# Attention and MoE on one core: the second, offset transpose of q becomes two copies that exchange partition halves

## The chip, the cores and the metric

The kernel runs on one core of one Trainium2 chip. The time is device microseconds of one execution. The profile is one execution of the program recorded by the hardware profiler; engines are named as in it: PE (matrix engine), PEld (its weight loads), DVE, ACT, POOL and SP. SP computes nothing here: it issues DMAs from its queue, one after the other, and an instruction that waits for a semaphore holds up all that stand behind it. PE, too, takes its instructions in the order in which they were written.

## The reference

Eight batches of twelve heads, 448 positions, head width 64; then one feed-forward layer over the 3584 rows that come out:

```python
scores = scale * np.matmul(q, k.transpose(0, 1, 3, 2))   # q, k, v: (8, 12, 448, 64), scale = 1/8
attn = np.maximum(scores, 0.0) ** 2 / S                   # S = 448, no softmax
x = np.matmul(attn, v)                                    # then (8*448, 768)
h = x @ w_in                                              # (768, 2048)
g = 0.5 * h * (1.0 + erf(h * inv_sqrt2))
out = g @ w_out                                           # (2048, 768)
```

Inputs and output are float32; the kernel computes with bfloat16 operands.

## The kernel before, in words

**Layout.** A batch `b` is worked on in three groups `g` of four heads. For the score products q and k must lie with the head width (64) on the partitions, so both are turned. Queries are loaded as 112 partitions with four chunks `c` of 64 columns each per head (`load_q`: row `p*4+c` of a head is chunk `c` of partition `p`); keys are loaded as 128 partitions. Batches 0 and 1 are turned on PE (`add_tk`, `add_tq`). Batches 2 to 7 are turned by DMA transposes on SP's queue (`add_T_dma`, line 660).

**The turned q, before.** One transpose takes 128 columns at a time, that is two chunks, and puts the first on partitions 0 to 63, the second on 64 to 127. A score product reads 64 partitions and must find all four chunks of a head there. So q is transposed twice per group: the "even" transpose starts at a chunk's edge, the "odd" one is offset by 64 columns. Both write into every other slot of `qT`, so that each half holds the four chunks side by side and a product reads one run of 448 columns (`moving = qT[r, n * KC : n * KC + S]`). The odd transpose reaches one chunk past its group, so it also waits for the next group's load; two memsets clear the two column blocks at q's ends. With one transpose of k that is nine transposes per batch, 54 in all (36 of q, 18 of k).

**Order.** Nothing is scheduled at run time. The string `ORDER` lists the operations of all engines, each word a letter for the engine (P = PE, A = ACT, D = DVE, G = POOL, S = SP) and a number (the operation's place in the order in which the code adds them). Each engine gets its words in that order. In batch 2 the nine operations 228 to 236 are k, q even, q odd of group 0 (228, 229, 230), of group 1 (231, 232, 233), and of group 2 (234, 235, 236). Written as k2.0 (batch 2, group 0) and so on, SP's queue before is

- q2.0 even, k2.0, q2.0 odd, k2.1, q2.1 odd, q2.1 even, q2.2 odd, q2.2 even, k2.2 (S229 S228 S230 S231 S233 S232 S236 S235, and S234 four lines further on).

**What waits for what.** A score block `(b, g, i)` (`fn_qk`, line 734, four products of 64x448) waits for its group's k and q transposes. There are seven blocks per group. P276 to P294 are the blocks of batch 2 group 0, P300 to P318 those of group 1, P324 to P342 those of group 2; PE runs them among feed-forward products (line 847, line 1259), in the order P285 (a block of group 0), P300, P303 (the first two of group 1). After each group come the products with v (line 795).

**Loads.** POOL issues all loads, in its own order, into one queue. Before loads that overwrite turned data POOL runs a *gate* (`add_gate`, line 701): a 16-column copy of `qT` that waits for the group's transposes, and so holds back the loads behind it. Around batch 2 POOL's order is: gate of group 0, two pieces of `w_out` (line 490), gate of group 1, a large piece of `w_out` (16 row blocks), then v, q of batch 3, **k of batch 2 group 2** (`G153`), and further loads. Each output block is stored by two DMAs on SP (line 1125), which stand in SP's queue between the transposes.

Of the kernel before, what the change touches and what calls it, by code (L numbers as in the profile page):

```python
# [9 lines left out]
BF16 = mybir.dt.bfloat16  # L10
AF = mybir.ActivationFunctionType

B, H, S, D = 8, 12, 448, 64
KC = 112
# [10 lines left out]
SLOTS = H * NC + 1  # L25
# [44 lines left out]
T_LOAD = 1.0  # L70

# [12 lines left out]
G0 G1 G3 G4 G1428 G7 G121 A10 P11 D13 G2 A16 P17 D12 P14 G117 D18 P42 P39 G6 P21 D15 P19 A43  # L84
G118 P36 D22 P33 A40 P23 G5 D20 P25 D41 P54 A37 G122 D24 Z1056 D26 A34 P66 P57 D38 A55 D44 G8
P63 P29 P27 A58 D67 P69 P51 D35 A64 P48 D30 P31 D65 A70 P45 D28 D32 A52 P78 D59 G9 P133 D46 A49
P108 D68 D47 P111 A79 P75 D134 P129 A109 D50 P81 P131 D56 A76 P102 D112 P84 G125 A82 D71 P72 D53
A103 G120 P60 D130 A85 D104 P93 A73 P135 A61 D110 A74 A62 P96 D132 P105 G124 P141 D83 D77 A97
P168 A94 D106 P165 P90 A142 G119 P143 D86 D113 A169 G126 D107 P114 A166 D80 P87 D98 A91 D95 P171
A144 D115 P137 A88 D92 A116 P99 D89 P156 A172 D136 P159 A100 D138 P145 G128 A157 A101 D160 P162  # L90
P186 D167 P174 A146 P251 D163 A175 P243 D158 A187 D176 G148 A252 D170 P183 P195 P189 G147 D173
A244 P259 G151 A196 D184 G154 P253 D161 A260 G150 D164 P139 A190 P198 A254 P180 P177 D140 A181
D199 P219 P216 P245 A178 G123 G127 A220 D217 P207 A179 P210 P204 D191 A246 P261 S229 A211 D208
P247 D182 A205 S228 D209 A262 D197 P213 P222 P192 D200 S230 A248 P263 D221 A223 D206 P249 D224
A264 D188 P255 D212 A250 P257 D193 A214 A256 D194 P265 D218 S231 A258 D185 P201 D215 A266 G237
S233 G239 P225 A202 S232 A203 P276 P279 P267 D226 S236 A277 A227 P291 D280 P288 P294 S235 A268
P356 G240 A295 D289 G238 P350 A357 G149 P348 G272 A292 A351 G153 P285 P300 P303 G270 A349 P354
G241 A301 P364 A304 A355 P312 P318 P362 A365 P370 D319 D281 A363 D296 P358 A313 D290 A286 P282
P306 A371 P315 P352 A359 D307 P360 A353 P376 A361 P368 A316 A377 D317 P372 D314 A369 D308 P366
D293 A373 P378 A283 A367 D284 P374 S234 A379 D390 P382 D278 S400 A375 D391 S402 D392 P380 D417  # L100
D418 D305 G242 G152 D302 S399 D287 G269 P327 P339 D320 P297 G271 D396 G155 A328 D383 P333 G274
P384 D381 G273 D298 A340 A299 D393 A334 D394 P330 P324 P309 D329 P387 D419 A331 D335 A385 S398
A310 D395 D311 S386 A325 P342 P336 S401 P321 D397 D388 A343 D332 P421 A322 D337 A323 S403 P423
D420 D338 D422 S406 P446 P443 D341 P449 P425 D424 D344 A450 S404 P427 G410 D444 G275 A426 G412
S405 D447 P429 D326 D428 P452 P455 P345 A456 D453 P440 P437 D445 P431 D430 A441 D560 P433 D346
A347 D432 P473 A438 P461 P470 D434 P509 G413 G407 G414 A471 D474 P513 D448 G409 A462 S545 D457
A510 G415 P479 D454 P476 P464 G408 A514 P519 D472 D442 G411 A465 D439 P517 A520 D477 P515 A480
D451 A518 S547 P485 P467 P458 S436 A468 P491 A516 S543 P511 D459 A486 D561 P523 S389 A492 D487
S549 A512 D460 P503 P494 P500 D563 A524 P525 D463 S541 A495 D466 P521 D469 A526 D481 P531 S548
D504 A522 D478 P527 A532 D501 P537 D475 S542 A528 D505 P529 D502 A538 D493 S546 P488 P497 P482  # L110
S544 A498 D489 P606 G556 P600 G550 G416 P535 A483 A530 G558 P533 D601 G551 A607 D484 A536 G553
D490 G552 P539 D496 G555 D499 P609 G559 P603 P506 G557 A604 D610 G554 P624 A534 P639 D562 P564
A540 D605 A507 P566 A640 D625 D565 D508 P615 P612 P618 D567 P568 A616 D613 P570 D617 A569 D611
D614 P572 S708 D619 P657 D571 P627 P636 S706 P574 D580 D573 A637 D620 P576 D608 A658 D575 S578
A628 P584 D581 S704 D638 D577 P586 D583 S579 D582 P630 D602 P633 P621 S707 D626 A634 D631 P651
A585 S710 P642 P588 D632 D587 A643 S705 D659 P590 D629 A652 A622 D641 P648 A623 D644 P666 P663
A589 S712 D653 P592 D635 D591 A664 S709 G713 P594 G714 A649 D667 D593 S711 P654 P660 P645 A655
D661 P769 P763 D595 P596 S598 D725 A770 G719 G721 A646 P672 D764 G715 D597 P674 G720 D665 D650
A673 G716 G717 A647 D656 P772 P778 P775 G718 D662 A675 P678 S867 A776 D779 P676 D668 A773 D771
P766 D777 P787 P669 S868 A767 D788 A679 P781 P790 A677 D774 P682 A670 D723 D768 P684 A782 A671  # L120
D724 A683 D765 P680 D783 A791 D780 P796 P799 P784 A681 S874 A800 D797 P793 P802 S435 P688 S869
D803 D804 S870 D798 D789 S872 D792 S873 S871 S875 G882 G722 A785 A685 P686 A794 A689 A786 P811
P823 P805 A687 P690 D795 A806 P692 A691 D824 P698 D726 A812 D807 A693 P696 D801 A699 P814 P817
P808 A697 A815 D818 P820 P906 G884 P694 A809 G876 G877 P702 D907 G883 A695 A810 G878 P700 G879
A821 G881 A703 P826 P829 D822 P912 A701 P727 A827 P729 D828 A728 D813 P731 A913 D730 A830 D816
P733 D819 D825 P921 D831 P909 P832 A910 D922 P918 P936 D732 G885 P735 D734 A833 G880 D911 A919
D834 P924 P915 A937 P737 D736 A916 D925 P930 P933 D938 P942 P739 D743 A931 D738 S741 D744 P747
A934 D745 D740 S742 P749 D917 S599 A748 D935 S979 P751 D914 A943 D920 D750 S983 P753 D944 A752
D746 S985 P755 D923 D926 D754 P757 D932 D908 S986 P939 P948 P927 D758 S978 A940 D949 P960 P945
D941 P835 A928 S980 D756 D950 A946 P759 A929 S761 D961 S982 D947 P957 P954 P951 A836 D760 S981  # L130
A958 D955 P963 P966 P839 D956 A952 S762 D953 S984 A967 P837 D959 A840 P969 D964 P972 P987 A838
D888 P841 A973 P843 D988 D965 A842 D989 P845 A970 D962 A844 D974 P847 D971 A846 D1067 P1002 D968
P990 P975 A1003 D991 A848 P993 P996 P851 D976 A994 A977 P999 D997 P1014 P1005 A852 D1004 P849
D995 D992 P853 D886 A850 D1068 P857 D998 A1000 A854 P855 D1015 A1006 D1001 P1017 D1007 P1026
P1008 D1070 A1027 D1018 P1029 A856 P1011 P859 A858 D1059 A1009 D1028 P863 D1019 A1030 A860 D1031
P865 A1012 D1060 A864 A1010 P1035 D887 P1047 P1020 D1016 A866 P861 A1048 P890 D1021 A1036 A862
D1063 D1022 P1023 P1041 P1044 A891 D1013 P892 A1024 D1042 P1053 A1045 D1025 P1050 P1032 D1069
A1051 D1054 P1038 P1071 A1033 D1062 P894 D1049 A1072 D1043 P1088 D893 A1039 P1073 A1034 D1066
A895 P1079 A1089 D1040 P1090 D889 P1096 P1075 D1091 P896 D1055 D1074 D1181 P1094 D1052 P1077
D897 P1092 P898 D1095 D1078 P1082 D1064 P1099 P900 D1061 D899 D1097 P902 D1083 D1100 P1105 D1080  # L140
D901 P1102 A1076 D1179 P1085 A1106 D1139 P1122 A1093 D1046 A1084 P1107 D1037 P1124 A1123 D903
S905 P1109 A1081 D1086 P1126 D1103 A1087 P1113 D1108 P1130 D1125 A1110 P1128 A1127 D1065 P1111
A1104 D1140 A1098 P1056 D1180 D1129 D1112 P1133 D1131 P1143 D1057 D1114 P1119 D1058 P1136 D1134
D1291 P1116 D1144 P1183 D1120 P1200 D1137 P1185 D1117 P1202 A1184 D1141 A1201 P1191 D1182 P1187
D1203 P1145 D1186 P1189 P1206 P1208 P1147 D1190 D1207 D1146 P1194 D1192 P1211 D1209 P1149 D1195
P1214 D1212 D1148 P1217 D1150 P1197 D1142 P1151 A1218 A1115 D1198 A1118 P1221 D1215 A1135 P1234
D1152 A1121 P1219 A1132 P1236 A1101 A1138 P1153 A1235 D1237 P1238 D1161 P1155 D1220 D1154 S1157
P1240 D1159 P1223 D1156 S1158 P1163 D1160 D1241 P1245 P1165 D1164 D1224 P1228 P1167 D1166 D1162
D1246 P1169 D1229 D1168 P1225 P1171 D1170 D1253 P1173 D1172 D1226 P1175 D1251 P1242 P1231 A1239
P1204 A1222 P1303 A1227 D1243 P1248 D1176 A1188 P1320 A1205 D1252 P1295 A1210 D1174 S1177 A1244  # L150
D1232 P1312 S904 A1199 D1292 P1255 S1178 A1230 D1249 A1296 D1254 A1313 P1297 D1293 A1193 P1314
A1196 P1299 A1256 P1257 A1233 D1298 A1213 D1315 A1216 P1301 P1316 D1258 P1318 P1261 D1319 P1259
D1302 D1304 D1294 P1309 D1262 P1323 A1260 A1250 P1263 D1310 A1247 D1324 P1306 D1321 P1265 D1264
D1307 P1326 P1329 P1346 D1327 P1331 D1271 P1267 A1347 D1272 A1330 P1350 P1348 D1268 P1333 P1275
D1349 D1266 S1269 D1273 P1277 S1270 D1276 P1279 D1274 D1332 D1278 P1352 P1335 A1280 P1281 P1283
# [239 lines left out]
def kernel(  # L395
# [59 lines left out]
    def q_cols(b):  # L455

        if b < 2:
            return nq[b]
# [1075 lines left out]
```

## Time and profile before

| | |
|---|---|
| runs, us | 371.06, 371.53, 376.39; median 371.53 |
| profiled execution, span from first to last instruction | 371.2 us |
| PE busy | 358.8 us (97%) |
| DVE busy | 288.0 us (78%) |
| ACT busy | 191.9 us (52%) |
| POOL busy | 63.8 us (17%) |
| DMA transposes of q / of k | 36 / 18, median issue 1.30 / 1.27 us |
| median issue to landing, q / k | 4.9 / 3.6 us |

The busy time of PE counts pipelined products with modelled ends, so it is read together with the waits of PE and not by itself. A DMA has two times: that of its issue on SP or POOL, and that from issue to landing, when the semaphore that others wait for is raised. The profiled span lies 0.3 us under the median of the runs, so times worked out from the profile stand for those of the runs almost as they are.

### The profile page before, as it was taken

What the parts mean: (1) busy time and instruction counts of PE and PEld (TensorE: products, weight loads), DVE (VectorE), ACT (ScalarE), POOL (GpSimd) and SP (SyncE); (2) the same over time, 40 slices, a digit from 0 to 9 for tenths busy, and PEclk for the clock granted to TensorE, in tenths of its full rate; (3) what the DMA queues carried; (4) which work ended last, traced back from release to release, by engine and by line L of the source; (5) the groups of instructions that cost most, each with busy time, mean ns of one, the idle gap of its engine ahead of it and who ended that gap; (6) DMA issues with size and microseconds to landing.
All of it is one profiled execution on the core that took longest, in us unless ns stands there. A gap on an engine that the chain in (4) does not pass through costs nothing.

```text
span 371.2 us, 8452 instructions
## 1 busy us (share of the span) xinstructions
PE 358.8 (97%) x3560; PEld 222.3 (60%) x3560; DVE 288.0 (78%) x480; ACT 191.9 (52%) x312; POOL 63.8 (17%) x103
## 2 busy tenths in 40 slices
PE   8889999989999999999998899999999999999995
PEld 7665654445544555544454444467898787867563
DVE  3999862588996899898577899999977866667663
ACT  4987867626377543678665366860514134232100
POOL 8565126200140240030060000000000000000000
PEclk9999999999999999999999999999999999999999
DMA  9999999999999999999999970000100204021224
GB/s 168 200 200 202 195 160 181 203 196 159 196 157 182 191 194 204 192 133 198 145 133 239 212 156 2 2 2 0 45 2 0 87 0 129 2 85 44 86 83 129
DMA packets 89541, 47.27 MB, mean 127 GB/s; under 512 B 55328, under 2 KB 86048, under 8 KB 89504
## 3 DMA queue, kind: packets, MB, share of 16 engines
q0 software_dynamic: 32912, 22.47, 42.7%
q1 hardware_dynamic: 55952, 23.76, 33.4%
q8 instruction: 28, 0.46, 0.5%
q10 hardware_dynamic: 640, 0.51, 0.4%
q14 instruction: 9, 0.07, 0.1%
HBM read 45.61 MB, written 11.01 MB: 153 GB/s over the span
## 4 chain that ended last, share of the span: by engine, by line
PE 73%; DMA 14%; DVE 5%; SPq 3%; POOL 2%; issue 1%; DVEq 0%; POOLq 0%
PE pso L1164 25%; PE psh L847 17%; PE pb L991 13%; PE pav L795 8%; PE ps L734 8%; DMA nk<-in_k_dram 4%; DMA out_dram<-osb 4%; SPq L660 3%; DMA kT<-nk 3%; DMA v_sb<-in_v_dram 2%; DVE osb L1198 2%; DVE a_sq L755 2%; PE pso L1259 1%; DMA qT<-nq 1%; DVE s_sb L1145 1%
## 5 line engine op out<-in xcount | busy, mean ns | idle before, releaser
L746 ACT ACTIVATE a_sq<-ps 128x896 bf16<-128x896 f32 (+1 forms) x116 | 102.5, 923 | 46.9 <-PE ps L734 43.9
L755 DVE TENSOR_TENSOR a_sq<-a_sq 128x896 bf16<-128x896 bf16 x169 | 97.0, 616 | 7.9 <-ACT a_sq L746 7.7
L847 PE MATMUL psh<-xT,win_sb 128*128 128x448 bf16 (+1 forms) x516 | 96.3, 340 | 0.0
L847 PEld LDWEIGHTS <-win_sb 128*128 128x128 bf16 x516 | 47.9, 98 | 46.1 <-issue 10.0
L748 DVE TENSOR_SCALAR a_sq<-ps 128x896 bf16<-128x896 f32 (+1 forms) x53 | 57.1, 1080 | 18.4 <-PE ps L734 18.1
L1164 PEld LDWEIGHTS <-s_sb 128*128 128x128 bf16 x424 | 40.7, 98 | 28.7 <-issue 4.8
L857 ACT ACTIVATE h_sb<-psh 128x448 bf16<-128x448 f32 x80 | 43.5, 550 | 22.0 <-PE psh L847 21.7
L734 PE MATMUL ps<-qT,kT 64*64 64x448 bf16 (+1 forms) x756 | 47.7, 336 | 2.5 <-DMA kT<-nk 1.4
L1028 DVE TENSOR_TENSOR part<-pb,part 128x448 f32<-128x448 f32 x60 | 35.3, 620 | 13.5 <-PE pb L991 11.4
L1164 PEld LDWEIGHTS <-h_sb 128*128 128x128 bf16 x312 | 29.7, 98 | 21.2 <-issue 3.6
L1164 PE MATMUL pso<-wout_sb,s_sb 128*128 128x384 bf16 (+2 forms) x216 | 38.1, 320 | 2.6 <-DVE osb L1198 2.6
L1164 PE MATMUL pso<-wout_sb,h_sb 128*128 128x384 bf16 x208 | 38.1, 327 | 0.0
L1164 PE MATMUL pso<-t_sb,s_sb 128*128 128x384 bf16 x208 | 38.1, 327 | 0.0
L795 PE MATMUL pav<-a_sq,v_sb 64*64 64x448 bf16 (+1 forms) x756 | 36.4, 329 | 1.4 <-issue 1.2
L1198 DVE TENSOR_TENSOR osb<-pso,p_sb 128x384 f32<-128x384 f32 x39 | 21.6, 554 | 16.5 <-PE pso L1164 8.9
L734 PEld LDWEIGHTS <-kT 64*64 64x64 bf16 x756 | 18.4, 105 | 22.4 <-issue 15.3
L991 PEld LDWEIGHTS <-win_sb 128*128 128x128 bf16 x288 | 27.5, 98 | 2.9 <-issue 0.7
L795 PEld LDWEIGHTS <-v_sb 64*64 64x64 bf16 x756 | 21.2, 107 | 13.0 <-issue 2.3
L1037 ACT ACTIVATE h_sb<-part 128x448 bf16<-128x448 f32 x36 | 18.4, 576 | 19.0 <-DVE part L1028 18.9
L513 ACT CAST xT<-pav 128x448 bf16<-128x448 f32 (+1 forms) x38 | 18.3, 500 | 7.8 <-PE pav L795 6.4
L701 POOL COPY gate<-qT 128x16 bf16<-128x16 bf16 x15 | 4.9, 325 | 97.0 <-DMA qT<-nq 95.6
L991 PEld LDWEIGHTS <-ws 128*128 128x128 bf16 x216 | 20.8, 98 | 1.2
(59 smaller groups left out, 298.2 us busy)
## 6 DMA issues: line engine op xcount, KB each, us to landing
nk<-in_k_dram POOLq DMA_DIRECT2D x23, 224.0 KB, 8.1
nq<-in_q_dram POOLq DMA_DIRECT2D x21, 224.0 KB, 8.3
v_sb<-in_v_dram POOLq DMA_DIRECT2D x5, 672.0 KB, 7.6
out_dram<-osb SPq DMA_DIRECT2D x8, 336.0 KB, 4.2
v_sb<-in_v_dram POOLq DMA_DIRECT2D x9, 224.0 KB, 9.4
out_dram<-osb SPq DMA_DIRECT2D x7, 288.0 KB, 2.7
out_dram<-osb SPq DMA_DIRECT2D x8, 240.0 KB, 4.2
win_sb<-in_moe_w_in_dram POOLq DMA_DIRECT2D x8, 192.0 KB, 8.9
```

What stands on the lines that cost most here:

```text
L734: nc.tensor.matmul(ps[64 * j : 64 * j + 64, e, x * w : x * w + w], kT[r, g, i * 128 + 64 * j : i * 128 + 64 * j + 64], moving, start=True, ...
L746: A.activation(ar, ps, AF.Relu, scale=c_att)
L748: V.tensor_scalar(ar, ps, c_att, 0.0, op0=mybir.AluOpType.mult, op1=mybir.AluOpType.max,)
L755: V.tensor_mul(box["a2"][:, :, :used], ar, ar)
L795: nc.tensor.matmul(pav[0][o2 : o2 + 64, e, :w], vt[b][r, 2 * g + e, bass.ts(i, D)], box["a2"][r, y, o : o + w], start=(i == 0), stop=(i == ...
L847: nc.tensor.matmul(ph[:, x * n : x * n + n], win_sb[:, kd, bass.ts(m + x, 128)], xT[b][:, kd, c], start=(kd == 0), stop=(kd == KD - 1),)
L857: A.activation(h_ring()[:, m : m + nm, o + c.start : o + c.stop], box[0][:, :S].rearrange("p (x n) -> p x n", x=nm), AF.Gelu,)
L991: nc.tensor.matmul(bank[name][:, y, z * HS : z * HS + HS], w[:, k, bass.ts(mm, 128)], right()[:, k], start=first and k == 0 and z == 0, st ...
L1028: V.tensor_add(get(to), ps(name), get(other))
L1037: A.activation(h_ring()[:, m : m + 2, o + half[c].start : o + half[c].stop], src().rearrange("p (x n) -> p x n", x=2), AF.Gelu,)
L1164: nc.tensor.matmul(box[bank][:, n0:n1], left()[:, kf], right()[:, kf, n0:n1], start=bool(need) and kf == 0, stop=kf == K2 - 1, skip_group_ ...
L1198: V.tensor_add(out()[:, n0:n1], box[bank][:, n0:n1], other()[:, n0:n1])
```

## The change

Per group of four heads the odd transpose goes. The even transpose now fills a segment of 896 columns (`q_seg(b, 2 * g)`): partitions 0 to 63 hold chunks 0 and 2 of the four heads, partitions 64 to 127 chunks 1 and 3. Two plain DMAs on SP, which wait for that transpose, then copy the upper half to the lower half of a second segment and the lower half to the upper half (64 partitions of 896 columns each). A score product reads its 448 columns as two pieces of 224, one in each segment (`q_pair`); the chunks come in the order 0, 2, 1, 3, which the store undoes (`ORDERS`). The gate waits for the even transpose alone, and so do loads that overwrite the untransposed q. The two memsets go. The padding and the wait for the next group's load go.

In `ORDER` the words of PE, ACT, DVE and POOL keep their sequence; words of SP move. 230, 233 and 236 are now the copies ("swaps", two DMAs each) of groups 0, 1 and 2. SP's queue in batch 2 becomes

- q2.0, k2.0, k2.1, q2.1, swap 2.0, q2.2, k2.2, swap 2.1, swap 2.2, q3.0 (S229 S228 S231 S232 S230 S235, then S234 S233 ahead of P285 P300 P303, then S236).

```diff
-P247 D182 A205 S228 D209 A262 D197 P213 P222 P192 D200 S230 A248 P263 D221 A223 D206 P249 D224
...
-P356 G240 A295 D289 G238 P350 A357 G149 P348 G272 A292 A351 G153 P285 P300 P303 G270 A349 P354
...
-D293 A373 P378 A283 A367 D284 P374 S234 A379 D390 P382 D278 S400 A375 D391 S402 D392 P380 D417
...
+S228 D209 A262 D197 P213 P222 P192 D200 S231 A248 P263 D221 A223 D206 P249 D224 A264 D188 P255
...
+P350 A357 G149 P348 G272 A292 A351 G153 S234 S233 P285 P300 P303 G270 A349 P354 G241 A301 P364
...
-                nc.gpsimd.memset(nq[b][:, :D], 0.0)
-                nc.gpsimd.memset(nq[b][:, D + H * NC * D :], 0.0)
...
+    def q_seg(b, n):
+
+        return get_T(b)[0][:, SEG * n : SEG * n + SEG]
+
+    def q_pair(b, g, e, o):
+
+        x = q_seg(b, 2 * g + e)[64 * e : 64 * e + 64, o : o + HS]
+        step = -SEG if e else SEG
+        return bass.AP(x.tensor, x.offset, [x.ap[0], (step, 2), x.ap[1]])
...
+        def swapped(g):
+            def fn(e):
+                src = q_seg(b, 2 * g)
+                to = q_seg(b, 2 * g + 1)
+                nc.sync.dma_start(to[:64], src[64:])
+                nc.sync.dma_start(to[64:], src[:64])
...
-            even = turn(slots_of(8 * g, 1, 8), q_src(8 * g, 1, 8), lands)
-            prior = odd or even
-            beyond = [ld_q[b, g + 1, c] for c in range(NC)] if g < G - 1 else []
-            beyond = list(dict.fromkeys(beyond))
-            odd = turn(slots_of(n0, 0, n - n0), q_src(n0, 0, n - n0), lands + beyond)
-            n0 = n
-            for c, o in enumerate((even, odd, prior, odd)):
-                Tq[b, g, c] = (o, o)
+            even = turn(q_dst(g), q_src(g), lands)
+            both = sch.add(
+                (("SP", SWAP_STEP, SWAP_TIME),), swapped(g), [even] + after.pop(0), mode="X"
+            )
+            for c in range(NC):
+                Tq[b, g, c] = (even, both)
...
-            n = (16 * g + 1) * KC
-            nc.gpsimd.tensor_copy(gate, get_T(b)[0][:, n : n + 16 * KC : KC])
+            nc.gpsimd.tensor_copy(gate, q_seg(b, 2 * g)[:, : SEG : SEG // 16])
...
-                                n = 4 * (4 * g + 2 * ((2 * i + e) // NK) + j) + 1 - e
-                                moving = qT[r, n * KC : n * KC + S]
+                                moving = q_pair(b, g, e, (2 * ((2 * i + e) // NK) + j) * HS)
...
+            k = ORDERS[bb > 1][k]
```

## The prediction

> **What bounds the kernel now.** I read the page's busy times first, then the waits of PE, then SP's, POOL's and PE's timelines around the one wait of PE that a transpose ends, then the chain through it.
>
> The page:
>
> ```profile
> span 371.2 us, 8452 instructions
> ...
> PE 358.8 (97%) x3560; PEld 222.3 (60%) x3560; DVE 288.0 (78%) x480; ACT 191.9 (52%) x312; POOL 63.8 (17%) x103
> ...
> q0 software_dynamic: 32912, 22.47, 42.7%
> q1 hardware_dynamic: 55952, 23.76, 33.4%
> ```
>
> The waits of PE (who waited, for whom: total us, times, longest):
>
> ```profile
> PE pso L1164 <- DVE osb L1198: 2.6, 2, 2.1
> PE ps L734 <- DMA kT<-nk: 1.4, 1, 1.4
> ```
>
> PE is the bound: it stands idle 12.4 us of 371.2, and no q transpose ends any of it; one k transpose ends 1.4 us. So whatever the change saves on DMAs can win a few us at most, and what matters is whether a product becomes late. The place is batch 2. SP's timeline (start, duration, both us):
>
> ```profile
> 48.36 1.42 SPq L660 DMA_TRANSPOSE kT<-nk  x1
> 49.83 7.92 SPq L660 DMA_TRANSPOSE qT<-nq  x4
> 73.91 1.27 SPq L660 DMA_TRANSPOSE kT<-nk  x1
> ```
>
> The four of q are q2.1 and q2.2, both transposes each. Then SP stands still from 57.8 to 73.9 us: k2.2 is next, and its load is not there. POOL and PE:
>
> ```profile
> 51.13 0.60 POOL L701 COPY gate<-qT 128x16 bf16<-128x16 bf16 x1 [11.63 <-DMA qT<-nq]
> 56.38 0.21 POOL L701 COPY gate<-qT 128x16 bf16<-128x16 bf16 x1 [3.20 <-DMA qT<-nq]
> 56.83 1.15 POOL L490 DMA_DIRECT2D wout_sb<-in_moe_w_out_dram  x1 [0.24 <-issue]
> 59.41 0.72 POOL L546 DMA_DIRECT2D nk<-in_k_dram  x1
> ```
>
> ```profile
> 60.20 0.76 PE L734 MATMUL ps<-qT,kT 64*64 64x448 bf16 x12
> 83.82 0.57 PE L734 MATMUL ps<-qT,kT 64*64 64x448 bf16 x8 [1.39 <-DMA kT<-nk]
> ```
>
> The load of k2.2 is issued at 59.41 behind the 1536 KB piece of w_out. The 12 products at 60.20 are P285, P300, P303: group 1 begins here. The 8 at 83.82 are the first of group 2. The chain (start, duration) joins load, transpose and product:
>
> ```profile
> 59.41 14.48 DMA nk<-in_k_dram
> 73.89 0.02 issue
> 73.91 9.88 DMA kT<-nk
> ```
>
> **The step that decides.** In the changed queue swap 2.1 stands behind k2.2, and P300 reads both halves that swap 2.1 makes. Before, P300 needed nothing behind k2.2. SP is in order, so swap 2.1 cannot be issued before k2.2's load has landed; PE is in order, so all work behind P300 waits, the 21.6 us of products that ran from 60.4 to 82.4 as cover for k2.2 among it.
>
> *When k2.2's load lands.* Three things move it. (1) The first gate waits for q2.0 and k2.0, no longer for the odd transpose: SP's first two transposes landed at 49.4 and 50.2 (42.03 plus 8.13), so it starts near 50.3 instead of 51.13: 0.8 us. The second gate now waits for the fourth DMA of the queue, which landed at 51.8 (48.36 plus 3.45), not 56.3, so the large piece is issued about 4.2 us earlier; but the queue ahead of it is not empty (the second small piece landed at 61.64), so that moves its place in the queue and not its end. (2) Three transposes fewer stand in these loads' way. The trace's packets of 256 bytes, the transposes' own, are 49,056 with a mean of 27.8 ns: over 54 transposes and 16 engines 1.58 us each, so 4.7 us. (3) The swap's two copies stand there in their place. No SBUF-to-SBUF copy is in the trace. One has 64 rows of 1792 bytes; packets of 896 bytes took 96.9 ns and of 3072 bytes 161.7 ns, so 64/16 packets take between 0.39 us (at 96.9) and 0.78 us (two of 896 per row); I take 0.7 as nearest to the 3072-byte row, 1.4 for the pair. Net 3.3 us of engine work. In 40 to 84 us the queues' shares add up to some 1.3 (two queues in flight at once), so 2.5 us of time. Sum: 0.8 + 2.5 = 3.3; load lands at 73.9 - 3.3 = 70.6. Bounds: 0.8 and 4.9.
>
> The Trainium skill, "Advanced Engine Details and Errata", section "X-Bar Transpose (TRN2)", says transposing DMAs are as fast as regular ones. By it the swap would cost as much as the transpose, 1.58 us, and the load would land 0.1 us later than in my sum; it speaks against the DMA saving, and no run here shows it yet.
>
> *When swap 2.1 lands.* k2.2 landed 9.88 us after issue because loads filled the engines; the loads behind it are as many as before, so I take the same: 80.5. Bounds 3.1 us (the k transpose issued at 125.75, no loads) and 12.4 (the q transpose at 76.16). The copies are issued 1.3 us behind k2.2 and follow it in its queue; their own issue is bounded by the stores' 0.32 to 1.36 us. The two stores issued behind k3.0 landed 0.9 and 1.05 us after it (95.08; 95.95 and 96.13): 1.0 more, 81.5.
>
> *What PE loses.* P300 started at 60.4 (60.20 plus one block of 0.19). Stall 81.5 - 60.4 = **21.1 us**. The wait at 83.82 goes, since k2.2 lies then 20 us ahead of its product: **-1.4**. After so long a gap PE's clock must be counted. At the program's start the 45 products of 128 columns on zeros ran 106 ns apart ((4.98 - 0.31)/44), the 48 products of 448 columns at 67.98 189 ns apart, or 54 ns per 128 columns: half pace for 5.0 to 6.3 us, from 0.99 until about 7. Before, the longest gap within the work was 2.1 us, and no slow products followed it. For a gap of 20 us the start of the program is the nearest row: half pace for 5.4 us loses **+2.7**. Bounds 0 and 3.2.
>
> The Trainium skill, "TensorE: Matmul & The Clock Gate", Part 1, gives the idle state 1.2 GHz after about 3.4 us idle and 2.4 GHz after about 3.4 us of sustained work. By it the restart would lose 1.7 us, the sum 1.0 less; the half pace agrees with the start here, its length does not.
>
> **The other edits.** Fifteen more odd transposes go (24 us of DMA work), 34 copies come; no PE wait ends on them, so 0. The two memsets took 0.17 us each, and POOL waited 1.14 us for a DMA right behind them: 0. The read in two pieces: the halves of batches 0 and 1 show its bound. 64x224 products, four at once, cost 0.19 us per two rounds (8 in 0.39, 16 in 0.58), one round of 64x448 0.19 (8 in 0.57, 12 in 0.76). Even as two products each, 126 rounds would lose under 0.5 us; below 0 nothing, since the same columns are read. I take 0.
>
> *Swaps behind stores, batches 3 to 7.* In batch 3 swap 3.0 now follows a store whose data came at 90.29, in batch 4 the one at 116.98, then one transpose; in 5, 146.37; in 6, 172.14; in 7, 202.43. Store, transpose and swap issue take 0.8 to 3.5 us, landing 3.1 to 5.7. At the worst rows swap 3.0 lands near 97.1, its product began at 96.48; batch 4: 126.8 against 127.08; 6: 181.6 against 181.61. Store data and products shift alike, while the loads run 20 us ahead: 0, bound +2.
>
> **Sum.** 21.1 - 1.4 + 2.7 = 22.4 us on the profiled 371.2; its median run is 0.3 longer: 371.5 + 22.4 = **394 us**. Low: load 4.9 us early (69.0), landing of k2.2 with half the loads gone (5.6, as k3.1 at 91.20), swap 1.0 behind: stall 15.2, clock 0: 385. High: load 0.8 early, landing 9.9, copies 2, clock 3.2, late swaps 2: 401.
>
> **Rivals.** *More than one stall* (chance 0.07). Swaps also come late in batches 4 or 6, where slack is under 1 us. For it: the queue is longer by 18 entries. Against: loads gain 20 us on the products. 401 to 410, say 405.
>
> *Not slower* (0.05). If swap 2.1 landed before P300, the change would only lose the 1.4 us wait: 370. One mechanism: the load of k2.2 comes early enough that SP passes it, which decides at 58 us (58 + 1.3 + about 1). For it: gates open earlier and transposes go. Against: the 1536 KB piece alone took 61.64 to 70.45.
>
> *The DMAs speed up as a whole* (0.06). With fewer small packets k2.2 lands 3.1 us after its issue: swap 2.1 near 75, stall 14.3, with clock 387, without 384. Against: loads, not transposes, fill the engines from 64 to 84 us.
>
> *The products read two pieces at half pace* would add 126 x 0.19 = 24 us, 418; the halves speak against it (0.01).
>
> **How the numbers follow.** Forecast 0.81, others 0.19. The likeliest is 394; 385 to 401 holds it and half of the third rival. About 2% (7.4 us) is what a measurement tells from no change. "Not slower" lies within it but for 0.01, since all of PE's waits on DMAs are worth less: faster 0.01, within 0.04, slower 0.95.
>
> **What would show it.** The profile after would have one PE wait of 15 to 25 us ahead of a score product near 60 us, ended by a DMA into qT, nothing at k2.2's product, a k2.2 issue at 69 to 73, products at half pace for some us after the gap, and no other PE wait over 2 us. Wrong it would be if SP issued swap 2.1 before k2.2's load landed, or if the gap ended by 66.

## The result, and the profile after

| | before | after |
|---|---|---|
| median of 4 runs each, us | 372.20 (371.06 to 376.39) | 395.26 (394.12 to 395.91) |
| after : before | | 1.057 [1.051, 1.062] |
| profiled span, us | 371.2 | 393.8 |
| PE busy, us | 358.8 | 362.9 |
| mean granted clock of PE | 1.00 | 0.966 |

The change makes the kernel 5.7% slower: 22.6 us by the two profiled spans. In all that follows the ratio with its interval counts and not the difference of medians, because the runs of the kernel before scattered from 370 to 383 us, and the ratios leave disturbed runs out and so differ from the quotients of the medians. A run takes about 2 us more than its own span (395.91 and 393.8 us for the profiled one after), so spans are compared with spans, and the span of 371.2 us stands for a run of about 373 us, not for the median of 371.5. From the page after (busy times, the granted clock in 40 slices of 9.85 us, the queues):

```profile
span 393.8 us, 8474 instructions
...
PE 362.9 (92%) x3560; PEld 222.8 (57%) x3560; DVE 288.0 (73%) x480; ACT 192.2 (49%) x312; POOL 64.7 (16%) x101
...
PEclk9999987559999999999999999999999999999998
...
q0 software_dynamic: 32912, 22.47, 40.0%
q1 hardware_dynamic: 41456, 23.59, 29.0%
```

PE's busy share falls from 97% to 92%, and its clock is low only in the sixth to the ninth slice, from 49 to 89 us, and at the very end. That points to batch 2. The transposes' queue carries 14,496 packets fewer for nearly the same bytes, and nothing of that is seen in the time. Waits of PE after (who waited, for whom: total us, times, longest):

```profile
PE ps L741 <- issue: 16.5, 1, 16.5
PE ps L741 <- DMA qT<-qT: 4.2, 2, 3.1
...
PE pso L1172 <- DVE osb L1206: 1.2, 2, 0.7
```

The 16.5 us are new, and so are the 4.2. "issue" says that the profile found no event that ended the wait, so the cause has to be read from the other engines. SP after (start, duration in us):

```profile
51.02 0.61 SPq L686 DMA_DIRECT2D qT<-qT  x1
...
52.35 1.62 SPq L666 DMA_TRANSPOSE qT<-nq  x1
73.13 1.22 SPq L666 DMA_TRANSPOSE kT<-nk  x1
74.41 0.58 SPq L686 DMA_DIRECT2D qT<-qT  x1
75.04 0.59 SPq L687 DMA_DIRECT2D qT<-qT  x1
```

Swap 2.0 goes out at 51.02, q2.2 at 52.35. Then SP stands still for 19 us, until the load of k2.2 has landed, and only behind k2.2 come the two copies of swap 2.1, which nothing but their place in the queue held back: q2.1, their source, was turned long before, at 52.73. The list of DMA issues from 74.3 to 74.5 us has the first of the two copies, with its size and the time from issue to landing:

```profile
qT<-qT SPq DMA_DIRECT2D x1, 112.0 KB, 9.3
```

Issued at 74.41, it landed at 83.71, and the second at 84.25. POOL after, with the load that SP waited for (`nk`), and PE after (the idle time before a group stands in brackets):

```profile
53.31 1.15 POOL L486 DMA_DIRECT2D wout_sb<-in_moe_w_out_dram  x1 [0.24 <-issue]
...
55.88 0.72 POOL L552 DMA_DIRECT2D nk<-in_k_dram  x1
```

```profile
55.35 0.38 PE L741 MATMUL ps<-qT,kT 64*64 64x448 bf16 x2 [1.10 <-DMA qT<-qT]
58.82 0.95 PE L741 MATMUL ps<-qT,kT 64*64 64x448 bf16 x6 [3.10 <-DMA qT<-qT]
...
83.80 1.45 PE L741 MATMUL ps<-qT,kT 64*64 64x448 bf16 x8 [16.54 <-issue]
...
88.61 0.57 PE L741 MATMUL ps<-qT,kT 64*64 64x448 bf16 x8
...
107.70 0.57 PE L741 MATMUL ps<-qT,kT 64*64 64x448 bf16 x8
```

The 8 products at 83.80 are P300 and P303, 0.09 us behind the landing of swap 2.1's first copy. They take 1.45 us; 8 of the same form at 88.61 take 0.57. Two things stretch them: P300's other two products start 0.49 us behind its first two, when the second copy has landed, and the products are slow, since the granted clock is half until 87.4. The first products of group 2 (107.70) wait for nothing; before, they waited 1.39 us for k2.2.

The delay adds up so, product by product against the trace before: P300 starts at 83.80 instead of 60.4, 23.4 us late. By 87.4, when the clock is full again, the lag has grown to 25.3: 0.5 by the wait for the second copy, 1.4 by the slow products (a run below measures this). The wait at k2.2's product is gone, 1.4, and a wait of 2.1 us at 205.3 for an output buffer is 0.7 now, 1.4. 23.4 + 0.5 + 1.4 - 1.4 - 1.4 = 22.5 of 22.6. The 0.1 that is left hides two small ones: 0.3 is made up in between, and 0.45 is lost at the end of the program.

### The profile page after: what moved, and what is told of

Same layout as the page of the kernel before. It is cut to its first block, busy times and chain, and to the rows that moved or that the text cites. A ratio compares the mean times of both kernels' runs of the same rounds, so it can differ in the third digit from the quotient of the medians.

```text
span 393.8 us, 8474 instructions
## 1 busy us (share of the span) xinstructions
PE 362.9 (92%) x3560; PEld 222.8 (57%) x3560; DVE 288.0 (73%) x480; ACT 192.2 (49%) x312; POOL 64.7 (16%) x101
## 4 chain that ended last, share of the span: by engine, by line
PE 78%; DMA 10%; issue 5%; POOL 3%; SPq 1%; DVE 1%; DVEq 0%; POOLq 0%
PE pso L1172 29%; PE psh L854 20%; PE pb L998 12%; PE ps L741 8%; PE pav L802 6%; DMA nq<-in_q_dram 5%; PE pso L1267 3%; DMA nk<-in_k_dram 3%; DMA qT<-qT 2%; SPq L666 1%; DVE osb L1206 1%; POOL nk L552 1%; POOL nq L463 1%; POOL v_sb L570 1%; DMA out_dram<-osb 1%
## 5 line engine op out<-in xcount | busy, mean ns | idle before, releaser
L854 PE MATMUL psh<-xT,win_sb 128*128 128x448 bf16 (+1 forms) x516 | 98.6, 345 | 0.3 <-DMA win_sb<-in_moe_w_in_dram 0.3
L755 DVE TENSOR_SCALAR a_sq<-ps 128x896 bf16<-128x896 f32 (+1 forms) x53 | 57.1, 1079 | 43.8 <-PE ps L741 43.5
L741 PE MATMUL ps<-qT,kT 64*64 64x448 bf16 (+1 forms) x756 | 49.7, 343 | 21.1 <-issue 16.5
L1172 PEld LDWEIGHTS <-h_sb 128*128 128x128 bf16 x312 | 29.8, 98 | 21.1 <-issue 3.4
L1206 DVE TENSOR_TENSOR osb<-pso,p_sb 128x384 f32<-128x384 f32 x39 | 21.6, 553 | 14.8 <-PE pso L1172 11.3
L802 PEld LDWEIGHTS <-v_sb 64*64 64x64 bf16 x756 | 21.1, 107 | 12.4 <-issue 1.2
L709 POOL COPY gate<-qT 128x16 bf16<-128x16 bf16 x15 | 6.1, 405 | 112.4 <-DMA qT<-nq 112.3
```

What stands on the lines that cost most here:

```text
L741: nc.tensor.matmul(ps[64 * j : 64 * j + 64, e, x * w : x * w + w], kT[r, g, i * 128 + 64 * j : i * 128 + 64 * j + 64], moving, start=True, ...
L755: V.tensor_scalar(ar, ps, c_att, 0.0, op0=mybir.AluOpType.mult, op1=mybir.AluOpType.max,)
L802: nc.tensor.matmul(pav[0][o2 : o2 + 64, e, :w], vt[b][r, 2 * g + e, bass.ts(i, D)], box["a2"][r, y, o : o + w], start=(i == 0), stop=(i == ...
L854: nc.tensor.matmul(ph[:, x * n : x * n + n], win_sb[:, kd, bass.ts(m + x, 128)], xT[b][:, kd, c], start=(kd == 0), stop=(kd == KD - 1),)
L1172: nc.tensor.matmul(box[bank][:, n0:n1], left()[:, kf], right()[:, kf, n0:n1], start=bool(need) and kf == 0, stop=kf == K2 - 1, skip_group_ ...
L1206: V.tensor_add(out()[:, n0:n1], box[bank][:, n0:n1], other()[:, n0:n1])
```

## The experiments

Eight kernels are variants of the changed one, one leaves its copies out, one is the kernel before with the new way of reading. The kernel before was run between them on the same chip each time, and each ratio is to these runs. Lines of `ORDER` are shown in part: each stands for a stretch of a longer line.

### Swap 2.1 ahead of k2.2

If the place of swap 2.1 in SP's queue is the whole matter, exchanging two words of `ORDER` ends the wait.

```diff
-P350 A357 G149 P348 G272 A292 A351 G153 S234 S233 P285 P300 P303
+P350 A357 G149 P348 G272 A292 A351 G153 S233 S234 P285 P300 P303
```

> The changed kernel with one pair of entries on SP's queue exchanged: swap 2.1 stands ahead of k2.2, not behind it. Theory (head of the line: swap 2.1 waits for k2.2's load only because it stands behind it): swap 2.1 is issued near 54.5 us and lands by 66, the 16.5 us gap ahead of P300 goes; the gap of 4.2 us ahead of group 0's products and its slow restart (2.3 us) stay, the wait at k2.2's product stays away. 375 to 378 us. Rival A (a copy needs 9 us and more wherever it stands, because loads fill the engines, or waits for something else): a gap of 5 us or more stays ahead of P300, 383 us or more. Rival B (the loss is spread, by the read in two pieces or by SP's longer queue): 390 us or more.

Measured: 379.04 us (10 runs) where the kernel before had 374.32, 1.014 [1.010, 1.018]; span 374.6. By the ratios three quarters of the loss are gone, 0.043 of 0.057. By the spans it is 19.2 of the 22.6 us, but the traced execution (376.56 us) is among the shortest of the ten. The time is 1 us over what was expected. SP and PE of this run:

```profile
52.40 0.60 SPq L686 DMA_DIRECT2D qT<-qT  x1
...
72.30 1.22 SPq L666 DMA_TRANSPOSE kT<-nk  x1
...
92.52 1.02 SPq L1133 DMA_DIRECT2D out_dram<-osb  x2
93.63 0.53 SPq L686 DMA_DIRECT2D qT<-qT  x1
```

```profile
63.53 0.38 PE L741 MATMUL ps<-qT,kT 64*64 64x448 bf16 x2 [2.07 <-issue]
...
100.72 1.26 PE L741 MATMUL ps<-qT,kT 64*64 64x448 bf16 x12 [1.95 <-issue]
```

Swap 2.1 goes out at 52.40 and k2.2 waits alone, until 72.30. P300 still waits 2.07 us, since the first copy takes 11.0 us to land among the loads. And a second wait of 1.95 us appears in batch 3, which the changed kernel did not have: swap 3.0 (93.63) stands behind an output block's store, which is not ready before 92.52, and its first copy lands 7.0 us after its issue. In the changed kernel swap 3.0 stands behind the same store, but PE was 20 us later against the loads: there the copy landed after 2.7 us, more than 2 us ahead of its product. The wait ahead of group 0, 4.2 us in the changed kernel, is 0.73 here although nothing ahead of it was moved, so it differs by some us from one execution to the next.

### k2.2's load ahead of the large piece of w_out

The same wait can be shortened from its other end: leave SP's queue as it is and let the load that its head waits for come earlier.

```diff
-G240 A295 D289 G238
-P350 A357 G149 P348 G272 A292 A351 G153 S234 S233 P285
+G240 A295 D289 G153 G238
+P350 A357 G149 P348 G272 A292 A351 S234 S233 P285
```

> The changed kernel with SP's queue as it is; on POOL the load of k2.2 is issued ahead of the 1536 KB piece of w_out, not three loads behind it. Theory (swap 2.1 waits for k2.2's load through SP's order): the load lands right behind the second small piece, near 62.6 instead of 73.1; k2.2 lands 9.7 later, near 72.3, swap 2.1 near 73.3, so P300 starts about 10.5 us earlier: 385 us. Rival A (the copies are late by themselves): P300 still near 83, 394 to 396 us.

Measured: 385.55 us, 1.026 [1.017, 1.034]; span 383.6. On SP and on PE of this run:

```profile
61.83 1.22 SPq L666 DMA_TRANSPOSE kT<-nk  x1
63.10 0.58 SPq L686 DMA_DIRECT2D qT<-qT  x1
```

```profile
72.28 1.58 PE L741 MATMUL ps<-qT,kT 64*64 64x448 bf16 x8 [7.51 <-issue]
```

k2.2 goes out 11.3 us earlier, P300 starts 11.5 us earlier, and the span falls by 10.2. The wait follows the load of k2.2 one for one, though P300 reads nothing of k2.2. Together with the first run this shows the chain: load, head of SP's queue, swap, product.

### The clock held up through the wait

Here 71 products on zeros are added between P285 and P300; their result is not used. They fill the wait, which itself stays.

```diff
-G0 G1 G3 G4 G1428 G7
+G0 G1 G3 G4 G1429 G7
...
-S234 S233 P285 P300 P303
+S234 S233 P285 Z36000 P300 P303
```

> The changed kernel with products on zeros (15 us of them at full pace, results unused) put ahead of P300, into the gap. Theory (a gap also costs a restart at half pace, about 1.8 us after P300): with PE kept busy the score products after the gap run at full pace, and the time falls by 1.5 to 2.5 us: 393 to 394 us. Rival C (the gap costs its own length alone, and the slow products behind it are covered): 395 to 396 us.

PE of this run:

```profile
67.21 15.47 PE L1505 MATMUL fill<-zero 64*64 64x512 bf16 x71
```

P300 starts at 83.02 and the granted clock is full from 64.4 on. From the start of P300 to that of group 2's first product the same work takes 22.62 us instead of 23.90, 1.28 less. Of the 22.62, P300's other half waits 0.65 for the second copy (83.02 to 83.67), where it was 0.49 in the changed kernel, so the low clock costs **1.4 us**, half of what was predicted. The times (394.71 us, 393.8 to 396.2; ratio 1.050 [1.041, 1.060]) cannot be told from those of the changed kernel and lie between the theory's and the rival's, so the 1.4 rests on the two traces alone.

### Each swap behind its own transpose

If every swap went out as soon as its source is turned, nothing would wait for a foreign load:

```diff
-D218 S232 A258 D185 P201 D215 A266 G237 S230 G239 P225
-A202 S235 A203 P276
...
-G153 S234 S233 P285 P300 P303
+D218 S230 S232 A258 D185 P201 D215 A266 G237 G239 P225
+A202 S233 S235 A203 P276
...
+G153 S234 P285 P300 P303
```

> The changed kernel with both swaps of batch 2 that were late moved: SP's queue is q2.0, k2.0, k2.1, swap 2.0, q2.1, swap 2.1, q2.2, k2.2, swap 2.2. Theory (both gaps are a matter of queue order): swap 2.0 lands near 53.5, swap 2.1 near 59, ahead of their products; no gap, no restart, the 1.4 us wait at k2.2 may come back because its product is at 83.8 again. 369 to 373 us, no different from the kernel before. Rival D (the waits for landings inside SP's queue hold up the transposes behind them): q2.2 or the gates behind q2.1 come late, another wait of 2 us or more appears, 374 us or more.

Measured: 382.69 us, 1.018 [1.007, 1.028]; span 381.1. The theory fell, and the rival by which the queue delays what follows held. SP and PE:

```profile
51.01 1.34 SPq L666 DMA_TRANSPOSE qT<-nq  x1
60.74 0.46 SPq L686 DMA_DIRECT2D qT<-qT  x1
...
79.07 1.22 SPq L666 DMA_TRANSPOSE kT<-nk  x1
```

```profile
90.03 1.64 PE L741 MATMUL ps<-qT,kT 64*64 64x448 bf16 x8 [4.37 <-DMA qT<-qT]
```

q2.1 goes out at 51.01, 1.35 us later than in the changed kernel (49.66), because swap 2.0 stands ahead of it. In between, at 50.41, the first loads of w_out are issued. q2.1 now takes 9.72 us to land instead of 3.07, so it lands 8.0 us later. Swap 2.1 waits for it at the head of SP's queue until 60.74, q2.2 goes out behind it, the second gate opens later (60.85 instead of 52.86), the load of k2.2 behind it lands later, and k2.2 goes out at 79.07 instead of 73.13. PE waits 3.19 us at P300, 4.37 at group 2 and 1.51 in batch 3. Swap 2.0 itself is in time here: group 0 does not wait at all.

### Swap 3.0 ahead of the store, too

The first run left a wait in batch 3, which its queue explains by the store. This takes it away (the exchange of 233 and 234 stays):

```diff
-S386 A325 P342 P336 S400 P321
+S400 S386 A325 P342 P336 P321
```

> As the run with swap 2.1 ahead of k2.2, and in batch 3 swap 3.0 stands ahead of the store that stood before it. Theory (in that run a gap of 1.95 us opened ahead of batch 3's first products because swap 3.0 stood behind a store whose data came late): that gap goes, the others (0.7 and 2.1 us in batch 2) stay: 1 to 3 us less than that run's 379.0, ratio to the kernel before 1.005 to 1.011. Rival (swap 3.0 is late because loads fill the engines): gap and time as in that run, 1.014.

Measured: 374.51 us (10 runs) where the kernel before had 376.64, **1.001 [0.997, 1.005]**; span 372.2. Swap 3.0 goes out at 88.38, the store at 92.76, and the wait in batch 3 is gone. What remains is 2.56 us ahead of group 0 (swap 2.0) and 0.70 at P300. Moving two words of an order of 1,429, with all operations of the change in place, takes the whole 5.7% back, more than was expected.

### Swap 2.1 directly behind swap 2.0

The same, with swap 2.1 ahead of q2.2 instead of behind it:

```diff
-A202 S235 A203 P276
+A202 S233 S235 A203 P276
...
-G153 S234 S233 P285
+G153 S234 P285
...
-S386 A325 P342 P336 S400 P321
+S400 S386 A325 P342 P336 P321
```

> As the run with swap 3.0 ahead of the store, and swap 2.1 stands directly behind swap 2.0, ahead of q2.2. Theory: swap 2.1 lands near 58, so the 2.1 us gap ahead of P300 goes too; left are the 0.7 us gap ahead of group 0 and perhaps the wait at k2.2's product, 1.4 us in the kernel before: 0.998 to 1.004 of the kernel before. Rival (every wait for a landing in SP's queue holds up what stands behind it, so q2.2, the third gate and k2.2 come late): a wait of 2 us or more at k2.2's product, 1.006 or more.

Measured: 374.98 us (12 runs), 1.006 [1.001, 1.011]; span 374.4. P300 and group 2 do not wait, but swap 2.0 lands late (0.52 and 2.26 us ahead of group 0), the granted clock is half from 58.1 to 61.5 us, and a later output buffer costs 0.89 us. The time is above what was expected, though the rival's wait at k2.2's product did not come. This place of swap 2.1 is not shown to be better than the last one.

### No copies at all

What is the exchange of 18 transposes for 36 copies worth by itself? Here all 36 copies are left out, and each product reads the 224 columns of the untouched segment twice, so its result is not the reference's. The work of PE is the same.

```diff
-        x = q_seg(b, 2 * g + e)[64 * e : 64 * e + 64, o : o + HS]
-        step = -SEG if e else SEG
+        x = q_seg(b, 2 * g)[64 * e : 64 * e + 64, o : o + HS]
+        step = 0
...
-                nc.sync.dma_start(to[:64], src[64:])
-                nc.sync.dma_start(to[64:], src[:64])
+                pass
```

> The changed kernel with all 36 copies left out; each score product reads the 224 columns of the even transpose's segment twice, so half of the chunks are not computed and the others twice. It prices the taking away of 18 transposes by itself. Theory (PE is the bound and no product waited for a q transpose): 368 to 372 us, 0.992 to 1.000 of the kernel before, since only the waits of 1.4 and 2.1 us can go. Rival (the transposes' DMA work held the loads up, and with them the products): 366 us or less, 0.987 or less. If the loss of the changed kernel were in the read of two pieces, this one would keep it: 394.

Measured: 370.60 us, 0.989 [0.982, 0.997]; span 367.6, and no wait in batch 2. So the transposes that the change removes are worth about 1%, and that is the most it could win with copies that cost nothing. By the spans it is 3.6 us, of which 2.8 are two waits of the kernel before: the 1.4 at k2.2's product, and 1.4 of the 2.1 for an output buffer.

### The kernel before, reading in two pieces

The kernel before keeps its transposes; its product reads the 448 columns as two pieces, the second half first, so the columns come in another order.

```diff
-                                moving = qT[r, n * KC : n * KC + S]
+                                y = qT[r, n * KC + HS : n * KC + S]
+                                moving = bass.AP(y.tensor, y.offset, [y.ap[0], (-HS, 2), y.ap[1]])
```

> The kernel before, in which each score product of batches 2 to 7 reads its 448 columns as two pieces of 224, the second half first (so the queries of those batches come out in another order). It prices the read alone. Theory: nothing, 0.997 to 1.003. Rival (a second piece costs a pass of its own): 126 rounds by 0.19 us, 24 us more, 1.06; by a start of a few ns per product, up to 2 us, 1.005.

Measured: 376.90 us (10 runs), 1.001 [0.995, 1.007]; span 371.3 against 371.2. Reading in two pieces costs nothing, as the products at 88.61 in the changed kernel already say (8 in 0.57 us, as before).

### The gates ahead of w_out

What is left of the best variant is swap 2.0's late landing. Swaps 2.1 and 3.0 stay as in the variant at 1.001; the two small pieces of w_out go behind the second gate, and k2.2's load ahead of the large one:

```diff
-D215 A266 G237 S230 G239 P225
+D215 A266 G237 S230 P225
...
-P356 G240 A295 D289 G238
-P350 A357 G149 P348 G272 A292 A351 G153 S233 S234 P285
+P356 G240 G239 A295 D289 G153 G238
+P350 A357 G149 P348 G272 A292 A351 S233 S234 P285
```

> The edit: swap 3.0 stands ahead of the store of group 1 (as in the run with the store behind), swap 2.1 ahead of k2.2 (as in the run with the swap first), and on POOL's queue the second gate goes ahead of the two small pieces of w_out and k2.2's load ahead of w_out's large piece. Theory: swap 2.0 lands late (55 to 58 us) because the pieces of w_out were issued at 50.4 us, in front of its packets; with them behind, the gap ahead of the first group of batch 2 (2.56 us in the run with the store behind) falls under 0.5 us, and with P300's 0.70 gone the time is about 2 us under that run's: ratio to the kernel before 0.993 to 0.998. Rival: the loads of w_out, now later, hold up the products that read them or the loads of batch 3, and a gap of 1 to 3 us appears near 77 us or at batch 3: ratio 1.0 to 1.008.

Measured: 373.85 us (12 runs) where the kernel before had 374.98, 0.998 [0.994, 1.002]. In batch 2 the theory holds: swap 2.0, which took 4.0 and 6.4 us to land in the variant at 1.001, takes 2.3 and 2.4 here, k2.2 goes out at 62.05, and no group of batch 2 waits. But a wait appears in batch 3. From the chain through it (start, duration) and from PE's timeline:

```profile
95.36 11.56 DMA qT<-qT
```

```profile
107.05 1.01 PE L741 MATMUL ps<-qT,kT 64*64 64x448 bf16 x12 [3.01 <-DMA qT<-qT]
```

Swap 3.1 needed 11.56 us from issue to landing, behind k3.2, q3.2 and a load of v. Part of the rival came true beside the theory. The trace is of the longest of the twelve executions (378.21 us, the median is 373.85), so whether the others have this wait is not shown.

### Swap 3.1 ahead of the store as well

```diff
-S400 S386 A325
+S400 S403 S386 A325
...
-A450 S403 P427
+A450 P427
```

(on top of the last one)

> The edit: the run with the gates first, and swap 3.1 moved from behind q3.2 to directly behind swap 3.0, ahead of the store, k3.2 and q3.2. In the run with the gates first swap 3.1 was issued at 95.36 us behind those two transposes and a v load of 672 KB (issued at 91.82), landed 11.56 us later, and the products of group 1 of batch 3 waited 3.01 us. Theory: issued near 90 us, ahead of that load, it lands before 100, the gap of 3.01 us goes, nothing takes its place, and the time is 370 to 372 where the kernel before has 375: ratio 0.988 to 0.994. Rival: what delays it is the traffic as a whole, and the store, k3.2 or q3.2, now two copies later, hold up an output block or group 2 by 1 to 3 us: ratio 0.995 to 1.002.

Measured: 373.63 us (12 runs) where the kernel before had 376.34, 0.997 [0.993, 1.001]; span 373.4. Swap 3.1 goes out at 89.82, and in this trace (375.63 us) the wait of 3.01 us is not there; no score product of batches 2 to 7 waits any more. The time did not fall to the expected 0.988 to 0.994. A wait of 2.03 us for an output buffer at 150.0 us and a half clock from 152.2 to 155.6 remain in the trace; the last run has the same pair at 151.6, so it comes with the wait of 3.01 us and without it. Neither variant is shown to beat the kernel before.

## Why the prediction was right

The step that was to decide did: swap 2.1 stands behind k2.2 in a queue that keeps its order, and P300 waits for it. The time (395.26 against 394) came out close partly by luck, because errors cancel. Of the 1.3 us between, 0.7 is the base: the median before was 372.2 and not 371.5. Term by term:

- **When k2.2's load lands.** Predicted 70.6, measured 73.1, just outside the 69 to 73 that the prediction named as its sign. The first gate opened at 50.13 (50.3 predicted) and the large piece was issued 3.5 us earlier (4.2 predicted), but the load came 0.8 us earlier and not 3.3. This is the term that was mis-sized, by 2.5 us. The loads ahead of it tell where the rest went: the second small piece of w_out was issued 1.3 us earlier, but landed at 61.44 instead of 61.64, and from there to the load of k2.2 it took 11.7 us instead of 12.3. Some of it may be this execution's own: the last two loads of v ahead of batch 2 landed 1.2 and 1.4 us later than in the profile before, and in two variants with the same loads, swap 2.1 ahead of k2.2, that transpose went out at 72.30 and 71.94, 1.6 and 2.0 us earlier than before the change. Even by these, about half of the 2.5 us for saved DMA work did not reach the load: a smaller sum of packets did not make the one load land as much earlier.
- **The price of a swap.** Predicted 1.4 us of engine work for the pair. The 2,304 packets of 1792 bytes took 120.9 ns on average: 128 packets over 16 engines, 0.97 us. A transpose has 896 packets at 28.2 ns, 1.58 us, the figure that the prediction took. But this mean holds stretches in which the transposes shared the engines with loads, up to 61.3 ns per packet from 57.1 to 64.3 us. Where no load moves, two transposes from 117.5 to 120.2 us have 21.2 ns, 1.19 us each, and the pairs of copies from 143.3 to 146.3 us have 129 and 133 ns, 1.03 and 1.06. By the Trainium skill, "Advanced Engine Details and Errata", section "X-Bar Transpose (TRN2)", transposing DMAs are as fast as regular ones; away from loads this trace agrees within some 15%. So about a quarter of the 1.58 came from sharing the engines. With 1.19 and 1.05 the 3.3 us of engine work that the prediction counts as saved would be 2.5, an estimate. What the saving is worth in time is the 1% of the run without copies, waits that go included.
- **When swap 2.1 lands.** k2.2 took 9.70 us (9.88 predicted), the copies followed it by 0.87 and 1.41 (1.0). Both held, because both came from rows with the same load traffic. The median over all 36 copies is 2.6 us, as the DMA issues of the page show:

```profile
qT<-qT SPq DMA_DIRECT2D x36, 112.0 KB, 2.6
```

- **What PE loses.** P300 late by 23.4 us (21.1 predicted, the 2.3 being the late load), the wait at k2.2's product gone (-1.4, right). The predicted single gap of 15 to 25 us came out as 16.5. The prediction missed that PE would be late already, by 4.2 us of waits for swap 2.0 and a half clock from 56.6 to 63.5: it put the 34 other copies at 0, and its sign "no other PE wait over 2 us" did not hold (3.1). It also missed the 0.5 us between the two copies. The wait for swap 2.0 cost nothing here, since P300 waits for a point in time; without the stall it is what is left ahead of group 0 in the variants, 0 to 2.8 us.
- **The clock.** Predicted +2.7 (0 to 3.2), measured 1.4, since the half pace lasted 3.55 us from P300's start and not 5.4. The Trainium skill, "TensorE: Matmul & The Clock Gate", Part 1, gives about 3.4 us of sustained work until full speed; its 3.4 was nearer than the start of the program, from which 5.4 was taken. The estimate of 1.7 us by it was 0.3 above the measured price. The start was a poor row: in the twelve traces of this case the clock becomes full at 3.6 to 6.9 us.
- **Terms of 0.** Two pieces: 0 (1.001 [0.995, 1.007]). Swaps behind stores: 0 in the changed kernel, but only because the stall moved PE; where the stall is gone it is 1.95 us, the predicted bound of 2.
- **Not foreseen:** the wait for an output buffer at 205.3 us shrank by 1.4 us. Together with the 1.3 us that the clock cost less than predicted it offsets the 2.3 us of the late landing and the 0.5 between the copies.

Of the rivals, "not slower" needed k2.2's load to let SP pass by 58 us; it came at 73.1. The variants with swap 2.1 ahead of k2.2 show what it would have given, 1.00 to 1.01. "More than one stall" was right in its mechanism and wrong in its place: a second wait over 2 us stood in batch 2 (3.1), and none in batches 3 to 7 of the changed kernel. "The DMAs speed up as a whole" is excluded by k2.2's 9.70 us from issue to landing, where it asked for 3.1. Half pace of the products is excluded by the run that reads in two pieces alone. The prediction also expected the profile to name a DMA into `qT` as what ended the wait; it named "issue", and the DMA was found by its landing time.

What stays open: why swap 2.0 and swap 3.1 need 7 to 12 us to land in one place and some 2.5 in another is laid to the loads around them by the runs that move loads or swaps, but which load's packets they stand behind was not measured.

## What to carry to other kernels

An entry of a DMA queue that waits passes its wait on to all that stand behind it: when a change gives an operation a new place in a queue, look up what it now stands behind, when that is released, and who waits for the operation. Here that place cost nearly all of the 5.7%. Two moved words took them back, and with these the change as a whole costs nothing that could be measured (1.001 [0.997, 1.005]). After a long stall goes, expect the waits it covered (2 us each here) to come out, and read the next one from the trace.

## What was not expected of the hardware

- The clock fell after much shorter gaps than the predicted long one. In the changed kernel there were waits of 1.10 and 3.10 us, with 0.4 us of work between, and the clock fell 0.9 us into the second, for 6.8 us; in the last variant a single wait of 2.03 us was followed by half clock for 3.4 us. Yet a wait of 2.1 us before the change, one of 2.56 us in the variant at 1.001 and one of 3.01 us in the variant with the gates first left the record at full clock. So the length of a wait alone does not decide it.
- The traces kept show what does. In each of the twelve the changes of the clock, from the first to the last, lie on a grid of steps of 3.413 us, which starts at another point in each execution; the stretches at half clock between two at full clock are 1, 2, 3 and 5 steps long (3.4, 6.8, 10.2 and 17.1 us). What counts is PE's idle time within one step, as the timelines give it. The clock fell at the end of all 21 steps at full clock with 2.01 us of it or more, and of none of the 1,266 with 1.99 or less. It became full after the 9 steps without any idle time, and not after the 9 with 0.54 or more. The 2.1 us before the change lay across two steps, 1.34 and 0.77; the 2.03 us in the last variant lay in one. This is read off after the fact, and no run was made to test it.
- A transpose issued 1.35 us later (51.01 instead of 49.66) landed 8.0 us later (60.73 instead of 52.73). The first loads of w_out were issued in between; that they are the cause is argued from that order, and from swap 2.0, which landed sooner (2.3 and 2.4 us) where these loads were moved behind it.
